# Moving the token scores and their softmax behind the output product, and transposing the memory 64 columns at a time, in a segmented memory-attention kernel

## The chip, the cores and the metric

The kernel runs on one core of one Trainium2 chip. The metric is the device time of one execution in microseconds (us): lower is better. The core's engines work at the same time, each through its own queue of instructions in order, and wait for one another by semaphores: TensorE (PE, with its weight loads shown apart as PEld), VectorE (DVE), ScalarE (ACT), GpSimd (POOL) and SyncE (SP), which issues most of the DMAs.

## The reference

Two blocks with a layernorm ahead of each and a residual around each: a memory-augmented attention that runs over segments in sequence, and a feed-forward block with a squared ReLU. Cut to what matters (S = 2048 tokens of width 640, 32 heads of 128, 8 memory rows, segments of 32 tokens, so 64 segments):

```python
for s in range(n_seg):
    h = concat([mem, x[s*32:(s+1)*32]])            # 8 memory rows and 32 tokens
    q, k, v = h @ Wq, h @ Wk, h @ Wv               # 32 heads
    scores = where(mask, q @ k.T * scale, -1e9)    # a memory row sees all 40, a token what is not behind it
    o = (softmax(scores) @ v) @ Wo
    mem = o[:8]                                    # feeds the next segment
    outs.append(o[8:])
h  = x + concat(outs)
h2 = h + relu(layernorm(h) @ w1 + b1)**2 @ w2 + b2
```

The eight memory rows of one segment's output are an input of the next segment, so the 64 segments form a chain.

## The kernel before, in words

All weights of the attention lie in SBUF. A block `b` is four segments; `step(b, sp)` does one segment `s = 4*b + sp`, 64 steps in all, and `for b ... for sp` at the end calls them. The order of the work on each engine is the order in which the code issues it (`tc.manual_schedule`): nothing is moved by a scheduler, so an instruction that waits holds up everything behind it on its engine.

A segment's rows are split. The memory rows and the first 24 tokens ("main", 32 rows) are projected in the step itself. The last 8 tokens of the four segments of a block ("tails") are projected ahead of time, as units of four matmuls kept in the list `fill`: ten units make one of q, k, v for a block, or (`wo_tail_units`) the output product of a block's tails. `run(fill, n)` issues the next n units; they also serve as work for TensorE while other engines finish something. `late`, `mid` and `win` are further lists: `late` holds work for the start of the next step (`flip`, the transpose of tail rows; `ln_stats`; the output of a tail product), `mid` layernorms, `win` 128-wide transposes on TensorE.

One step issues, in this order:

- up to three entries of `late`; on VectorE these stand ahead of the step's own transposes.
- `project`: q and k of head half 0, then of half 1 (20 matmuls each, L206), copied out by ScalarE (L222, L224, L403) and transposed into `qT` and `kT` by VectorE (`flip`, L227, and L406). `spread` copies the memory columns of `qT` into `qz` on GpSimd (L372, L374).
- `scores(0)` and `soft1(0)`: the memory rows' scores of half 0 (L414, L419) and the first part of their softmax. They read `qz` and `kT`.
- v of half 0 (`ps0`), with `token_scores(0)` (L487 the mask, L491) between its second and third chunk; then two chunks of v of half 1 (`ps1`), `scores(1)`, `token_scores(1)`, `soft1(1)`.
- `token_values` of the segment before (L353, L358), `values(0)` (L447, L452) and its copy by VectorE (L213), the remaining three chunks of `ps1`, `soft2(1)`, then on VectorE the token softmax's maximum `mxk` (L525) and difference `tk` (L527).
- the output product `pw` (`wo_rounds`, L238, 16 rounds of four matmuls): rounds 0 to 5, `values(1)` and its copy by ScalarE (L215), rounds 6 and 7, one unit of `fill`, rounds 8 to 15.
- the rest of the token softmax: `ek` (ScalarE, L540), `zk` and `rk` (VectorE, L542, L544), the products `pkt` and `pk` (GpSimd, L546, L549).
- `wo_out`: `otmp` (ScalarE, L245) and `o` (VectorE, L246); `token_out`: two copies by ScalarE (L363) and one by GpSimd (L365); `store_main`; an entry of `win`; four or six units of `fill`.
- `mem_to_hT`: the memory rows of `o` are transposed by 20 matmuls of 32 columns into `pm` (L316) and copied into the next step's `hT4` (VectorE, L318). The next step's projections wait for this.
- `tails_in`: GpSimd copies the next segment's tails into `qT` (L323) and `kT` (L325).
- two entries of `mid`, the rest of `fill`; then VectorE transposes `pkt` and `pk` (`pTt` L567, `pTk` L573) with two products on GpSimd between them (`pTx`, L570). The next step's `token_values` reads them.

The pools matter as follows. `mm` has three PSUM buffers, used in turn by every projection, by the token scores `sk` and by the units. `chn` has one, shared by `sm`, `pw` and `pm`. `rowtile` gives four row buffers in turn. The difference `tk` and `otmp` share one buffer (tag "tk").

After the steps comes the feed-forward part, in four blocks of 512 tokens (L813 to L857), which the change does not touch but for a buffer that it borrows earlier (`ht0[3]`).

Of the kernel before, what the change touches and what calls it, by code (L numbers as in the profile page):

```python
# [8 lines left out]
ACT = mybir.ActivationFunctionType  # L9
ALU = mybir.AluOpType  # L10
AX = mybir.AxisListType
F32 = mybir.dt.float32
BF16 = mybir.dt.bfloat16
# [3 lines left out]
def kernel(  # L17
# [16 lines left out]
    nc = tc.nc  # L34
    _, S, D = A_x.shape
    _, H, E = A_Wq.shape
    M = A_mem0.shape[1]
    SEG = 32
    G = 4
    HG = H // G  # L40
    HE = H * E
    EG = HE // G
    DC = D // 128
    DH = D // 2
    NB = S // 128
    NS = S // SEG
    HD = 24
    TL = SEG - HD
    NK = SEG + M
# [4 lines left out]
    scale = float(E) ** -0.5  # L54
# [13 lines left out]
    s1 = ctx.enter_context(tc.tile_pool(name="s1", bufs=1))  # L68
    s2 = ctx.enter_context(tc.tile_pool(name="s2", bufs=2))
# [5 lines left out]
    wv = wts.tile([128, DC * HE], BF16)  # L75
    wo = wts.tile([128, H, D], BF16)

    ident = const.tile([128, 128], BF16)
# [6 lines left out]
    mask = const.tile([128, HG, SEG], BF16)  # L85
# [15 lines left out]
    qT = const.tile([128, H, NK], BF16)  # L101
    kT = const.tile([128, H, 2 * SEG], BF16)
# [33 lines left out]
    for ch in range(2):  # L136
        nc.scalar.dma_start(out=o0[32 * ch:32 * ch + M, :].rearrange("m (c f) -> m c f", f=64),
                            in_=A_mem0[0].rearrange("m (c t f) -> t m c f", t=2, f=64)[ch])
# [22 lines left out]
    hT4s, hTts, tails = {}, {}, {}  # L161
# [34 lines left out]
    def proj(w, by, lhs, n, ps, c0, c1):  # L196

        if by == "columns":
            wr = w[:].rearrange("p (c g j n k e) -> p c n k g j e", c=DC, g=G, n=2, j=4, k=4)
        elif by == "half":  # L200
            wr = w[:].rearrange("p (c k j n e) -> p c n k j e", c=DC, k=G, n=2, j=4)
        else:
            wr = w[:].rearrange("p (c k n f) -> p c n k f", c=DC, k=G, n=2)
        for c in range(c0, c1):
            for k in range(4):
                nc.tensor.matmul(ps[32 * k:32 * k + 32, :], lhsT=lhs(c), rhs=wr[:, c, n, k], start=(c == 0), stop=(c == DC - 1))  # L206

    def mmtile():
        return mm.tile([128, 512], F32, tag="mm", name="ps")
# [31 lines left out]
    def wo_out(pw):  # L241
        o = o_ring[0]
        o_ring.append(o_ring.pop(0))
        tmp = s1.tile([128, DH], F32, tag="tk", name="otmp")
        nc.scalar.copy(out=tmp[0:64], in_=pw[64:128, 0:DH])  # L245
        nc.vector.tensor_tensor(out=o[0:64], in0=pw[0:64, 0:DH], in1=tmp[0:64], op=ALU.add)  # L246
        return o

    fill, late, mid, win = [], [], [], []

    def run(q, n):
        while n > 0 and q:
            q.pop(0)()
            n -= 1
# [57 lines left out]
    def mem_to_hT(o, hT4, sp):  # L312
        pm = chn.tile([128, 512], F32, tag="ch", name="pm")
        for c in range(DC):
            for q in range(4):
                nc.tensor.matmul(pm[32 * q:32 * q + 32, c * M:(c + 1) * M], lhsT=o[:, (2 * c + q % 2) * 32:(2 * c + q % 2 + 1) * 32],  # L316
                                 rhs=ident[:, q // 2 * 32:q // 2 * 32 + M], start=True, stop=True)
        nc.vector.tensor_copy(out=hT4[:, :, sp, 0:M], in_=pm[:, 0:DC * M].rearrange("p (c m) -> p c m", m=M))  # L318

    def tails_in(b, sp, which="qk", h0=0, h1=H):  # L320
        q, k = [tails[b][w][:].rearrange("p h (k s) -> p h s k", s=4)[:, h0:h1, sp, :] if w in which else None for w in "qk"]
        if "q" in which:
            nc.gpsimd.tensor_copy(out=qT[:, h0:h1, SEG:NK], in_=q)  # L323
        if "k" in which:
            nc.gpsimd.tensor_copy(out=kT[:, h0:h1, SEG:2 * SEG].rearrange("p h (j k) -> p h j k", k=TL),  # L325
                                  in_=k.unsqueeze(2).to_broadcast([128, h1 - h0, 4, TL]))
# [11 lines left out]
    def store_main(o, s):  # L338
        for ch in range(2):
            nc.sync.dma_start(out=o_all[s * SEG:s * SEG + HD, ch * DH:(ch + 1) * DH],  # L340
                              in_=o[32 * ch + M:32 * ch + 32, :])
# [19 lines left out]
    def token_out(s, po):  # L361
        for n in range(2):
            nc.scalar.copy(out=oTg[:, n, :, :, M:NK],  # L363
                           in_=po[:, :, n * 128:(n + 1) * 128].rearrange("p g (j q) -> p g j q", q=32))
        nc.gpsimd.tensor_copy(out=oTts[s // 4 % 2][:, :, s % 4 * TL:(s % 4 + 1) * TL], in_=oT[:, :, 32:NK])  # L365
# [12 lines left out]
    def step(b, sp, v=None):  # L378
        s = b * 4 + sp
        last = s == NS - 1  # L380
        hT4 = hT4s[b]
        lhs = lambda c: hT4[:, c, sp, :]
# [95 lines left out]
        if not ready:  # L478
            ps0 = mmtile()
            proj(wv, "half", lhs, 0, ps0, 0, 2)  # L480
        sk = mmtile()
        skv = sk[:, 0:HG * NK].rearrange("p (i k) -> p i k", k=NK)

        def token_scores(n):
            if n == 0:
                for g in range(G):
                    nc.tensor.matmul(skv[32 * g:32 * g + 32, :, M:NK], lhsT=ident[:, 0:32], rhs=mask[:],  # L487
                                     start=True, stop=False, skip_group_check=True)
            for j in range(4):
                for g in range(G):  # L490
                    nc.tensor.matmul(skv[32 * g:32 * g + 32, n * 4 + j, :], lhsT=qT[:, n * 16 + g * 4 + j, M:NK],  # L491
                                     rhs=kT[:, n * 16 + g * 4 + j, 0:NK], start=False, stop=(n == 1 and j == 3),
                                     skip_group_check=True)

        token_scores(0)
        if ready:
            run(fill, DC)
        if not ready:
# [3 lines left out]
            pT0 = soft2(0)  # L502
        if not ready:
            ps1 = mmtile()
            proj(wv, "half", lhs, 1, ps1, 0, 2)
        if not last:
            scores(1)
        token_scores(1)
        if not last:
            soft1(1)  # L510
        if ready:
            run(fill, DC)
        po = pop.tile([128, G, 512], F32, tag="po", name="po")
# [3 lines left out]
            values(0, pT0, po)  # L517
            values_out(0, po)
        if not ready:
            proj(wv, "half", lhs, 1, ps1, 2, DC)  # L520
            nc.scalar.copy(out=v[:, 512:1024], in_=ps1[:])  # L521
        if not last:
            pT1 = soft2(1)
        mxk = s1.tile([128, HG], F32, tag="mxk", name="mxk")
        nc.vector.tensor_reduce(out=mxk[:], in_=skv, op=ALU.max, axis=AX.X)  # L525
        tk = s1.tile([128, HG, NK], F32, tag="tk", name="tk")
        nc.vector.tensor_tensor(out=tk[:], in0=skv, in1=mxk[:].unsqueeze(2).to_broadcast([128, HG, NK]), op=ALU.subtract)  # L527

        pw = chn.tile([128, 512], F32, tag="ch", name="pw")
        main = lambda p: oT[:, p, 0:32]  # L530
        wo_rounds(main, pw, 0, 6)
        if not last:
            values(1, pT1, po)
            values_out(1, po)
        wo_rounds(main, pw, 6, 8)
        run(fill, 1)
        wo_rounds(main, pw, 8, 16)

        ek = s1.tile([128, HG, NK], BF16, tag="ek", name="ek")
        nc.scalar.activation(out=ek[:], in_=tk[:], func=ACT.Exp, scale=1.0)  # L540
        zk = s1.tile([128, HG], F32, tag="zk", name="zk")
        nc.vector.tensor_reduce(out=zk[:], in_=ek[:], op=ALU.add, axis=AX.X)  # L542
        rk = s1.tile([128, HG], F32, tag="rk", name="rk")
# [3 lines left out]
                                op=ALU.mult)  # L547
        pk = s1.tile([128, HG, 32], BF16, tag="pk", name="pk")
        nc.gpsimd.tensor_tensor(out=pk[:], in0=ek[:, :, 0:SEG], in1=rk[:].unsqueeze(2).to_broadcast([128, HG, SEG]),  # L549
                                op=ALU.mult)  # L550

        o = wo_out(pw)
        if s:
            token_out(s - 1, po)
        if s > 1:
            store_main(o, s - 2)
        outs = [win.pop(0)()] if win else []
        for f in outs:
            f()
        if not last:  # L560
            run(fill, 4 if outs else 6)
            mem_to_hT(o, hT4s[(s + 1) // 4], (s + 1) % 4)
            tails_in((s + 1) // 4, (s + 1) % 4)
        run(mid, 2)
        run(fill, 100)
        pTt = s1.tile([128, 2, 32], BF16, tag="pTt", name="pTt")
# [2 lines left out]
        for u in range(2):  # L569
            nc.gpsimd.tensor_tensor(out=pTx[:, u], in0=pTt[:, u, HD:32].unsqueeze(1).to_broadcast([128, 4, TL]),  # L570
                                    in1=same[:], op=ALU.mult)
# [39 lines left out]
    f1T = ck(FC * NT).rearrange("p (c t) -> p c t", c=FC)  # L611
    hnT0 = const.tile([128, DC, NT], BF16, name="hnT0")
    ht0 = [const.tile([128, D], BF16, name="ht0%d" % k) for k in range(NK4)]
    parked = [hnT0[:, c, :] for c in range(DC)] + [ht0[k][:, 0:512] for k in range(3)]
    hnTs = [hnT0[:], ck(DC * NT).rearrange("p (c t) -> p c t", c=DC)]
    ots = [ck(D) for _ in range(4)]
# [114 lines left out]
    for b in range(NB):  # L731
        for sp in range(4):
# [45 lines left out]
            if 2 <= e <= NK4 + 1:  # L778
                late.append(lambda e=e: prep_stats0(e - 2))
                mid.append(lambda e=e: prep_norm0(e - 2))  # L780
            step(b, sp, v0 if b + sp == 0 else None)

    def end_output(s):
# [10 lines left out]
    po = pop.tile([128, G, 512], F32, tag="po", name="po")  # L794
# [7 lines left out]
    for t in range(S // NT):  # L802
# [6 lines left out]
        for fc in range(FC):  # L809
            ps = mmtile()  # L810
            for c in range(DC):
                if fc < FFULL:
                    nc.tensor.matmul(ps[:], lhsT=w1[:, c, fc * 128:(fc + 1) * 128], rhs=hnT[:, c, :],  # L813
                                     start=(c == 0), stop=(c == DC - 1))
                    continue
                for hh in range(2):
                    nc.tensor.matmul(ps[FREM * hh:FREM * (hh + 1), 0:HT], lhsT=w1[:, c, fc * 128:F],
                                     rhs=hnT[:, c, HT * hh:HT * (hh + 1)], start=(c == 0), stop=(c == DC - 1))
# [4 lines left out]
            if more and fc >= 1 and (fc - 1) // 3 < NK4:  # L823
                k, stage = divmod(fc - 1, 3)
# [10 lines left out]
        for q in range(NK4):  # L835
# [6 lines left out]
            for hh in range(2):  # L842
                k = pr + 2 * hh
                for fc in range(FFULL):
                    nc.tensor.matmul(y[:, hh, 0:DH], lhsT=f1T[:, fc, k * 128:(k + 1) * 128], rhs=w2[:, fc, cs],  # L845
                                     start=(fc == 0), stop=False, skip_group_check=True)
                if more and q and (hh == 0 or q == 1):
                    k = q if hh == 0 and q > 1 else hh
                    prep_pe(t + 1, k, hn_[k])()
            for hh in range(2):  # L850
                r = slice(FREM * hh, FREM * (hh + 1))
                nc.tensor.matmul(y[:, hh, 0:DH], lhsT=f1T[r, FFULL, pr * 128:(pr + 1) * 128], rhs=w2[r, FFULL, cs],
                                 start=False, stop=True, skip_group_check=True)
# [40 lines left out]
```

## Time and profile before

| | |
|---|---|
| median of 3 runs | 1033.69 us (1029.55 to 1035.87) |
| the profiled execution's own time | 1031.81 us |
| its span, first to last instruction | 1029.7 us |
| granted TensorE clock, mean | 0.997 |
| PE busy | 970.4 us (94%) |
| DVE, ACT, POOL busy | 618.2 us, 533.9 us, 312.2 us |
| one step in the middle of the run | some 13 us |

How to read it: the profile is one execution on the chip. An instruction has a start and a duration; matmuls are pipelined, so a next one starts before the last has ended and the busy time counts both as one stretch. A group of instructions of one line, engine, operation and shape has a busy time, a mean duration in ns and the engine's idle time just before, with what ended it. In the timeline, "x20" are 20 instructions merged into one row, whose duration goes from the first's start to the last's end. A matmul's shape reads rows*columns of the stationary operand, then partitions x elements of the moving one: 128*32 128x512 takes 128 rows by 32 columns of weights. Line numbers are those of the listing above.

### The profile page before, as it was taken

The numbers are of one execution on the slowest core, as the hardware profiler recorded it, in microseconds if no ns is written. First come the engines' busy times: TensorE is split into PE (matmuls) and PEld (weight loads), VectorE is DVE, ScalarE is ACT, GpSimd is POOL, SyncE is SP. The second block draws the span as 40 slices with busy tenths as digits, with TensorE's granted clock in tenths as the row PEclk, the third lists the DMA queues.
The fourth block names the chain that finished last, engine by engine and source line by source line (L and its number), as shares of the span: only waits on it lengthen the run. The fifth ranks groups of instructions, "written<-read, shape, count | busy, mean of one in ns | idle before, by whom it ended". The sixth has DMA issues, their size and how long they took to land.

```text
span 1029.7 us, 58960 instructions
## 1 busy us (share of the span) xinstructions
PE 970.4 (94%) x26951; PEld 573.9 (56%) x26960; DVE 618.2 (60%) x1740; ACT 533.9 (52%) x1229; POOL 312.2 (30%) x807
## 2 busy tenths in 40 slices
PE   5779899999999999999999999999999999999998
PEld 2345455655655555565655665555566565555555
DVE  2156666766666766666666666666666676466432
ACT  3336555555555655555655555555555555533431
POOL 1123333333333333333333232323332333433210
PEclk9999999999999999999999999999999999999999
DMA  9960101000101010000000000000000110612200
GB/s 356 385 193 26 23 7 31 7 25 6 35 7 29 7 36 12 22 15 26 16 22 14 19 23 14 22 14 26 15 21 8 47 34 7 208 50 65 77 26 26
DMA packets 39144, 51.58 MB, mean 50 GB/s; under 512 B 6192, under 2 KB 34992, under 8 KB 36976
## 3 DMA queue, kind: packets, MB, share of 16 engines
q1 hardware_dynamic: 37936, 47.29, 13.9%
q8 instruction: 210, 3.44, 1.4%
q0 software_dynamic: 320, 0.26, 0.1%
q14 instruction: 38, 0.31, 0.1%
q10 hardware_dynamic: 640, 0.27, 0.1%
HBM read 38.37 MB, written 9.44 MB: 46 GB/s over the span
## 4 chain that ended last, share of the span: by engine, by line
PE 86%; DMA 6%; issue 2%; DVE 2%; SPq 2%; ACT 1%; ACTq 0%; DVEq 0%; POOL 0%; POOLq 0%
PE ps L206 47%; PE pw L238 15%; PE y L845 5%; PE ps L813 4%; PE ps L238 3%; PE po L447 2%; PE po L353 2%; PE sm L419 2%; DMA wq<-in_B_w_dram 1%; DMA vt_d<-row 1%; SPq L146 1%; DMA wv<-in_A_Wv_dram 1%; PE ps L491 1%; DMA wo<-in_A_Wo_dram 1%; PE pm L316 1%
## 5 line engine op out<-in xcount | busy, mean ns | idle before, releaser
L206 PEld LDWEIGHTS <-hT 128*32 128x32 bf16 x7680 | 193.2, 96 | 183.6 <-issue 19.6
L238 PE MATMUL pw<-wo,oT 128*32 128x320 bf16 x4224 | 185.2, 300 | 8.0 <-issue 3.6
L206 PE MATMUL ps<-wv,hT 128*32 128x512 bf16 x2520 | 171.3, 379 | 3.1 <-issue 2.5
L206 PE MATMUL ps<-wq,hT 128*32 128x512 bf16 x2520 | 159.2, 381 | 4.9 <-DVE hT L318 4.9
L206 PE MATMUL ps<-wk,hT 128*32 128x512 bf16 x2520 | 158.6, 380 | 0.1
L238 PEld LDWEIGHTS <-oT 128*32 128x32 bf16 x4224 | 106.7, 96 | 59.2 <-issue 12.1
L222 ACT ACTIVATE row<-ps 128x512 bf16<-128x512 f32 x156 | 93.3, 599 | 75.0 <-PE ps L206 74.5
L227 DVE STREAM_TRANSPOSE qT<-row 128x512 bf16<-128x512 bf16 x128 | 90.3, 705 | 65.8 <-ACT row L222 65.7
L546 POOL TENSOR_TENSOR pkt<-ek,rk 128x64 bf16<-128x64 bf16 x64 | 19.0, 296 | 360.6 <-DVE rk L544 360.6
L224 ACT CAST row<-ps 128x512 bf16<-128x512 f32 x115 | 68.0, 591 | 31.5 <-PE ps L206 31.3
L372 POOL COPY qz<-qT 128x96 bf16<-128x96 bf16 x126 | 33.7, 267 | 138.2 <-DVE qT L227 136.3
L325 POOL COPY kT<-kTt 128x1024 bf16<-128x1024 bf16 (+1 forms) x65 | 71.9, 1106 | 10.6 <-DVE kTt L227 10.6
L206 PEld LDWEIGHTS <-hTt 128*32 128x32 bf16 x1920 | 54.0, 97 | 32.1 <-issue 2.6
L245 ACT COPY otmp<-pw 64x320 f32<-64x320 f32 x66 | 27.9, 423 | 82.4 <-PE pw L238 82.4
L363 ACT CAST oT<-po 128x512 bf16<-128x512 f32 x128 | 68.7, 589 | 1.6
L246 DVE TENSOR_TENSOR o<-pw,otmp 64x320 bf16<-64x320 f32 x66 | 31.8, 482 | 62.5 <-ACT otmp L245 62.5
L521 ACT CAST v<-ps 128x512 bf16<-128x512 f32 x63 | 36.9, 586 | 60.7 <-PE ps L206 60.7
L227 DVE STREAM_TRANSPOSE kT<-row 128x512 bf16<-128x512 bf16 x65 | 46.1, 709 | 32.1 <-ACT row L224 32.1
L542 DVE TENSOR_REDUCE zk<-ek 128x8 f32<-128x320 bf16 x64 | 31.1, 486 | 50.9 <-ACT ek L540 50.9
L845 PE MATMUL y<-wq,wk 128*128 128x320 bf16 x416 | 61.2, 299 | 0.2
L403 ACT CAST row<-ps 128x256 bf16<-128x256 f32 x126 | 40.7, 375 | 30.0 <-PE ps L206 30.0
L500 ACT CAST v<-ps 128x512 bf16<-128x512 f32 x63 | 36.9, 586 | 30.3 <-PE ps L206 30.3
(114 smaller groups left out, 1630.2 us busy)
## 6 DMA issues: line engine op xcount, KB each, us to landing
wv<-in_A_Wv_dram SPq DMA_DIRECT2D x5, 1024.0 KB
wq<-in_A_Wq_dram SPq DMA_DIRECT2D x5, 1024.0 KB
wk<-in_A_Wk_dram SPq DMA_DIRECT2D x5, 1024.0 KB
vt<-vt_d SPq DMA_DIRECT2D x60, 64.0 KB
xt<-in_A_x_dram SPq DMA_DIRECT2D x20, 160.0 KB
vt_d<-row SPq DMA_DIRECT2D x22, 128.0 KB
wo<-in_A_Wo_dram SPq DMA_DIRECT2D x2, 1280.0 KB
wo<-in_A_Wo_dram SPq DMA_DIRECT2D x4, 640.0 KB
```

Source lines behind the costliest of these rows:

```text
L206: nc.tensor.matmul(ps[32 * k:32 * k + 32, :], lhsT=lhs(c), rhs=wr[:, c, n, k], start=(c == 0), stop=(c == DC - 1))
L222: nc.scalar.mul(out=row, in_=ps, mul=scale)
L224: nc.scalar.copy(out=row, in_=ps)
L227: nc.vector.transpose(out=dst[:, n * 16:(n + 1) * 16, 0:32], in_=row.rearrange("p (h e) -> p h e", e=32))
L238: nc.tensor.matmul(pw[32 * j:32 * j + 32, 0:DH], lhsT=lhs(p), rhs=wov2[:, head(p), ch], start=(h == 0), stop=(h == 15))
L325: nc.gpsimd.tensor_copy(out=kT[:, h0:h1, SEG:2 * SEG].rearrange("p h (j k) -> p h j k", k=TL), in_=k.unsqueeze(2).to_broadcast([128, h1 - ...
L363: nc.scalar.copy(out=oTg[:, n, :, :, M:NK], in_=po[:, :, n * 128:(n + 1) * 128].rearrange("p g (j q) -> p g j q", q=32))
L403: nc.scalar.copy(out=row[:, u * 256:(u + 1) * 256], in_=ps[:, u * 256:(u + 1) * 256])
L500: nc.scalar.copy(out=v[:, 0:512], in_=ps0[:])
L521: nc.scalar.copy(out=v[:, 512:1024], in_=ps1[:])
L813: nc.tensor.matmul(ps[:], lhsT=w1[:, c, fc * 128:(fc + 1) * 128], rhs=hnT[:, c, :], start=(c == 0), stop=(c == DC - 1))
L845: nc.tensor.matmul(y[:, hh, 0:DH], lhsT=f1T[:, fc, k * 128:(k + 1) * 128], rhs=w2[:, fc, cs], start=(fc == 0), stop=False, skip_group_chec ...
```

## The change

- `mem_to_hT`: ten matmuls with 64 columns of weights each, in place of 20 with 32.
- The token scores of both halves are issued together, behind `values(1)` and rounds 6 and 7 of the output product, where one unit of `fill` stood; that unit is now issued behind the output product with the others. `ps1` issues three chunks ahead of `scores(1)` and two behind `values(0)` (before: two and three).
- `mxk` and `tk` follow the token scores. `tk` has a buffer of its own, borrowed from `ht0[3]` and later from the pool of tail columns.
- `ek` stands behind `otmp` and ahead of `token_out` on ScalarE. `tails_in` stands ahead of the units and `mem_to_hT`. `zk`, `rk`, `pkt` and `pk` stand behind `mem_to_hT`, so on GpSimd behind `token_out`'s copy and `tails_in`, and on VectorE behind the copy of `pm`.

```diff
     def mem_to_hT(o, hT4, sp):
         pm = chn.tile([128, 512], F32, tag="ch", name="pm")
         for c in range(DC):
-            for q in range(4):
-                nc.tensor.matmul(pm[32 * q:32 * q + 32, c * M:(c + 1) * M], lhsT=o[:, (2 * c + q % 2) * 32:(2 * c + q % 2 + 1) * 32],
-                                 rhs=ident[:, q // 2 * 32:q // 2 * 32 + M], start=True, stop=True)
+            for ch in range(2):
+                nc.tensor.matmul(pm[64 * ch:64 * ch + 64, c * M:(c + 1) * M], lhsT=o[:, c * 64:(c + 1) * 64],
+                                 rhs=ident[:, 32 * ch:32 * ch + M], start=True, stop=True)
...
-        sk = mmtile()
-        skv = sk[:, 0:HG * NK].rearrange("p (i k) -> p i k", k=NK)
-
-        def token_scores(n):
...
+        def token_scores(skv):
...
-        token_scores(0)
...
-            proj(wv, "half", lhs, 1, ps1, 0, 2)
+            proj(wv, "half", lhs, 1, ps1, 0, 3)
         if not last:
             scores(1)
-        token_scores(1)
-        if not last:
             soft1(1)
...
-            proj(wv, "half", lhs, 1, ps1, 2, DC)
+            proj(wv, "half", lhs, 1, ps1, 3, DC)
             nc.scalar.copy(out=v[:, 512:1024], in_=ps1[:])
         if not last:
             pT1 = soft2(1)
-        mxk = s1.tile([128, HG], F32, tag="mxk", name="mxk")
-        nc.vector.tensor_reduce(out=mxk[:], in_=skv, op=ALU.max, axis=AX.X)
-        tk = s1.tile([128, HG, NK], F32, tag="tk", name="tk")
-        nc.vector.tensor_tensor(out=tk[:], in0=skv, in1=mxk[:].unsqueeze(2).to_broadcast([128, HG, NK]), op=ALU.subtract)
...
         wo_rounds(main, pw, 6, 8)
-        run(fill, 1)
+        sk = mmtile()
+        skv = sk[:, 0:HG * NK].rearrange("p (i k) -> p i k", k=NK)
+        token_scores(skv)
+        mxk = s1.tile([128, HG], F32, tag="mxk", name="mxk")
+        nc.vector.tensor_reduce(out=mxk[:], in_=skv, op=ALU.max, axis=AX.X)
+        if s == NS - 7:
+            tks.append(s2.tile([128, 2 * HG * NK], BF16, tag="hTt", name="tk")[:])
+        tk = tks[-1].bitcast(F32).rearrange("p (i k) -> p i k", k=NK)
+        nc.vector.tensor_tensor(out=tk, in0=skv, in1=mxk[:].unsqueeze(2).to_broadcast([128, HG, NK]), op=ALU.subtract)
         wo_rounds(main, pw, 8, 16)
-
+        o = wo_out(pw)
         ek = s1.tile([128, HG, NK], BF16, tag="ek", name="ek")
-        nc.scalar.activation(out=ek[:], in_=tk[:], func=ACT.Exp, scale=1.0)
+        nc.scalar.activation(out=ek[:], in_=tk, func=ACT.Exp, scale=1.0)
+        if s:
+            token_out(s - 1, po)
+        if s > 1:
+            store_main(o, s - 2)
+        if not last:
+            tails_in((s + 1) // 4, (s + 1) % 4)
+        outs = [win.pop(0)()] if win else []
+        for f in outs:
+            f()
+        if not last:
+            run(fill, 4 if outs else 6)
+            mem_to_hT(o, hT4s[(s + 1) // 4], (s + 1) % 4)
         zk = s1.tile([128, HG], F32, tag="zk", name="zk")
...
-        o = wo_out(pw)
-        if s:
-            token_out(s - 1, po)
-        if s > 1:
-            store_main(o, s - 2)
-        outs = [win.pop(0)()] if win else []
-        for f in outs:
-            f()
-        if not last:
-            run(fill, 4 if outs else 6)
-            mem_to_hT(o, hT4s[(s + 1) // 4], (s + 1) % 4)
-            tails_in((s + 1) // 4, (s + 1) % 4)
         run(mid, 2)
         run(fill, 100)
...
+    tks = [ht0[3][:]]
```

More of the change, by code (lines that the diff above doesn't have):

```diff
@@ L480, in step @@
             proj(wv, "half", lhs, 0, ps0, 0, 2)
-        sk = mmtile()
-        skv = sk[:, 0:HG * NK].rearrange("p (i k) -> p i k", k=NK)
-        def token_scores(n):
-            if n == 0:
-                for g in range(G):
[L487 to L492, printed above, removed]
+        def token_scores(skv):
+            for g in range(G):
+                nc.tensor.matmul(skv[32 * g:32 * g + 32, :, M:NK], lhsT=ident[:, 0:32], rhs=mask[:],
+                                 start=True, stop=False, skip_group_check=True)
+            for i in range(HG):
+                n, j = i // 4, i % 4
+                for g in range(G):
+                    nc.tensor.matmul(skv[32 * g:32 * g + 32, i, :], lhsT=qT[:, n * 16 + g * 4 + j, M:NK],
+                                     rhs=kT[:, n * 16 + g * 4 + j, 0:NK], start=False, stop=(i == HG - 1),
                                      skip_group_check=True)
-        token_scores(0)
         if ready:
```

## The prediction

> **What bounds the kernel now.** I read the page first: busy times, then the chain that ended last.
>
> ```profile
> PE 970.4 (94%) x26951; PEld 573.9 (56%) x26960; DVE 618.2 (60%) x1740; ACT 533.9 (52%) x1229; POOL 312.2 (30%) x807
> ...
> PE 86%; DMA 6%; issue 2%; DVE 2%; SPq 2%; ACT 1%; ACTq 0%; DVEq 0%; POOL 0%; POOLq 0%
> ```
>
> TensorE sets the time: 94% busy, 86% of the chain. The other engines have slack on average, but every step has places where TensorE needs what they have just made. So I took one step out of the timeline, engine by engine, and measured from W, the start of the last matmul of the output product. TensorE first (508.13 + 0.84 less the 0.299 of one matmul gives W = 508.67):
>
> ```profile
> 508.13 0.84 PE L238 MATMUL pw<-wo,oT 128*32 128x320 bf16 x17
> 508.73 1.53 PE L206 MATMUL ps<-wk,hTt 128*32 128x512 bf16 x24
> 510.06 0.29 PE L316 MATMUL pm<-ident,o 128*32 128x8 bf16 x19
> ...
> 515.18 0.19 PE L419 MATMUL sm<-kT,qz 128*32 128x64 bf16 x2
> ```
>
> `scores(0)` (L419) start at W+6.51 (6.54 in most steps of this kind). They need the first q and k flips of VectorE:
>
> ```profile
> 510.47 0.20 DVE L318 CAST hT<-pm 128x40 bf16<-128x40 f32 x1 [0.47 <-PE pm L316]
> 510.59 0.23 DVE L567 STREAM_TRANSPOSE pTt<-pkt 128x64 bf16<-128x64 bf16 x1
> 510.74 0.40 DVE L573 STREAM_TRANSPOSE pTk<-pk 128x256 bf16<-128x256 bf16 x1
> 511.11 1.30 DVE L227 STREAM_TRANSPOSE kTt<-row 128x512 bf16<-128x512 bf16 x2
> 512.78 0.71 DVE L227 STREAM_TRANSPOSE qT<-row 128x512 bf16<-128x512 bf16 x1 [0.37 <-ACT row L222]
> 513.85 0.71 DVE L227 STREAM_TRANSPOSE kT<-row 128x512 bf16<-128x512 bf16 x1 [0.35 <-ACT row L224]
> ```
>
> The k flip ends at 514.56, 0.6 us before its use. That slack is the number to keep. `pTt` and `pTk` stand ahead of all flips and wait for nobody, since GpSimd has made `pkt` and `pk` long before:
>
> ```profile
> 508.83 0.30 POOL L546 TENSOR_TENSOR pkt<-ek,rk 128x64 bf16<-128x64 bf16 x1 [5.23 <-DVE rk L544]
> 509.09 0.62 POOL L549 TENSOR_TENSOR pk<-ek,rk 128x256 bf16<-128x256 bf16 x1
> 510.64 0.40 POOL L365 COPY oTt<-oT 128x256 bf16<-128x256 bf16 x1 [0.94 <-ACT oT L363]
> 510.98 0.42 POOL L323 COPY qT<-qTt 128x256 bf16<-128x256 bf16 x1
> 511.35 1.12 POOL L325 COPY kT<-kTt 128x1024 bf16<-128x1024 bf16 x1
> ```
>
> **The change part by part.** *Token softmax behind the tails.* In the changed order GpSimd does L365, L323, L325 and only then `pkt` and `pk`; VectorE does the copy of `pm`, `zk`, `rk`, then `pTt` (waits for `pkt`), `pTk` (waits for `pk`), then the flips. ScalarE does `otmp`, `ek`, then `token_out`:
>
> ```profile
> 509.06 0.42 ACT L245 COPY otmp<-pw 64x320 f32<-64x320 f32 x1 [1.13 <-PE pw L238]
> 509.51 1.07 ACT L363 CAST oT<-po 128x512 bf16<-128x512 f32 x2
> ```
>
> `token_out` ends at W+1.91 now. `ek` (0.473 by its group's mean) goes ahead of it: W+2.38, or W+2.28 if its start overlaps by 0.10 as successive ScalarE instructions do at L363 (two of 0.589 in 1.07). L365 starts 0.06 later; from its start to the end of L325 it is 1.83 (510.64 to 512.47); then `pkt` 0.26 to the start of `pk`, and 0.62; then 0.03 for the semaphore and 0.40 for `pTk`. VectorE is free at W+5.43 to W+5.57; I take 5.5 against 2.48 now. `zk` and `rk` (0.49 + 0.20 after the copy of `pm`, some W+2.7) and the layernorms of `mid` (0.6) lie beside this and cost nothing; without that cover they would cost their 0.7 us.
>
> Behind `pTk` on VectorE stand the entries of `late`, the q flip and the k flip. Back to back the latter two take 1.25 (0.64 to the next start, 0.71 less an overlap), and 0.04 passes to TensorE. TensorE for its part arrives at 6.54 + 0.22 (the unit of `fill` now behind the product, one round of four matmuls: the six rounds at 508.73 start some 0.22 apart) + 0.18 (shapes, below) = W+6.9. By the kind of step that follows:
>
> - two tail flips in `late` (1.27): 5.5 + 1.27 + 1.25 + 0.04 = W+8.06, so `scores(0)` come 1.52 later than now.
> - `ln_stats` in `late` (0.93 from the end of `pTk` to the next flip, in a step at 863 us): W+7.72, against 6.54 where ten units fill the end and 6.38 where five do: 1.18 and 1.34 later.
> - a tail product's `o` (0.45): W+7.2, before TensorE arrives: no wait.
>
> *The rest of the step, `scores(0)` to W.* The token scores are the same 36 matmuls: 0.21 + 0.11 now, 0.32 together. The unit that leaves the product takes 0.22 out. One chunk of v (0.22) and `token_scores(1)` (0.11) no longer stand between `scores(1)` and the product's start. `values(0)` begin 0.11 earlier, and from their last matmul's start (505.24) to the end of the VectorE copy L213 (505.82) and its semaphore it takes 0.64; two chunks (0.43) and a shape change (0.11 from start to start) cover 0.55. A new wait of 0.09. Sum: -0.22 + 0.09 = -0.13 a step. `values(1)` keep some 0.2 of slack; the copy L215 is covered by the token scores, 0.31 where the unit gave 0.22. `mxk` and `tk` (0.94) end 0.15 before `otmp`. SP's queue holds only `store_main` here, in unchanged order.
>
> *Memory transposes.* 20 matmuls take 0.13 us (510.06 to 510.19): either 6.5 ns each, and ten take 0.065, or 26 ns a round on each column strip, and the five rounds remain. The saving is 0 to 0.065; I take 0. (The Trainium skill, TensorEngine Tiling (Array Packing), section Instruction Overhead, says each matmul has about 60 cycles of overhead, so that one column costs what 60 do; by that five rounds remain and nothing is saved.) Against it stands the new shape, 128*64 among 128*32. The feed-forward part shows a change of width and back:
>
> ```profile
> 913.69 1.03 PE L813 MATMUL ps<-hnT,wq 128*128 128x512 bf16 x4
> 914.64 0.74 PE L817 MATMUL ps<-hnT,wq 128*64 128x256 bf16 x10
> 915.31 0.58 PE L845 MATMUL y<-wq,wk 128*128 128x320 bf16 x3
> ```
>
> L813's last start is 914.34, and L817 comes 0.30 later where 0.216 is the spacing; back, 0.21 where 0.107 is. So 0.09 a change, two a step: 0.18, from 0 (a narrower change may cost nothing) to 0.20. (The same page, section Key Properties, says that changing the tiling mode drains the engine; by that the 0.18 is paid, and the trace agrees with 0.09 each.) Where TensorE waits at `scores(0)` anyway, this is inside the wait.
>
> **Sum.** 28 steps behind tail flips: 1.52 - 0.13 = 1.4 each, 39.2. Three of them have `ln_stats` too, 2.7 more. Nine times 1.21 and five times 1.05 for `ln_stats` alone: 16.1. Thirteen steps without a wait: 0.18 + 0.09 = 0.27 each, 3.5. The seven at the ends, likewise: some 4.5. Together +66 us. On the profiled execution's own 1031.8 (span 1029.7 and 2.1 around it) this is 1098; the median of the runs is 1.9 higher.
>
> **The rivals.** *(1) The late flips find cover, and only small costs remain* (chance 0.13): if GpSimd's spans, rough in any profile, are shorter than shown, VectorE must be free by W+6.9-0.04-1.25-1.27 = 4.3 for no wait. Then each of 63 steps pays 0.27: 1049. Against it: L365 to L325 takes 1.8 to 1.95 in every steady step. *(2) Not slower* (0.07): the chain ends by 4.3 and the narrower shape change is free as well. Then half the transposes save 0.065 x 64 = 4, and ten steps with five units, where TensorE waits for `o`, gain their unit's 0.22: some 1026. It needs 1.2 us off a chain whose instructions are all in the trace. *(3) A second wait at `scores(1)`* (0.12): behind a late k flip come the q flip (0.64), `mx`, and two k flips, ending 1.6 after it; `scores(1)` come 1.88 after it. Above 0.25 more, say GpSimd's `qz` late behind `pTx`, and 40 steps pay 0.5 each: 1118. *The transposes as such doing nothing* is already in my sum.
>
> **How the numbers follow.** The forecast (0.68) is 1098, its own range 1079 to 1110: 0.07 either way on 49 steps, and below by up to 15, as the 15.5 us that TensorE idles by "issue" may go into the new waits. The range reaches towards (1) and over (3): 1062 to 1118. The runs before spread by 6 us, so about 1% (10 us) can be told from no change. Faster by more than that 0.03, within it 0.06 (the rest of (2) and a little of (1)), slower 0.91.
>
> **What would show it.** In the changed profile: `pkt` waiting not for `rk` but starting as L325 ends; `pTt` idle behind `pkt`; no gap between `pTk` and the flips; TensorE idle some 1.2 us at L419 in steps behind tail flips and about none at a block's first step; L213 ahead of L238 with 0.1; L316 preceded and followed by 0.09. I am wrong if VectorE's flips start where they do now, or if L419 shows no idle time.

## The result, and the profile after

The changed kernel takes 1098.73 us (median of 4 runs, 1095.19 to 1099.2) against 1032.01 before; the ratio is 1.0636, with a 95% interval of 1.0614 to 1.0658. The median before moved between 1027 and 1035 us from one batch of runs to another, so below every kernel is given with its ratio to the kernel before in the same batch.

The page of the changed kernel, busy times and the chain that ended last:

```profile
span 1097.1 us, 57756 instructions
...
PE 996.7 (91%) x26320; PEld 584.2 (53%) x26320; DVE 606.2 (55%) x1740; ACT 538.4 (49%) x1229; POOL 309.4 (28%) x807
...
PE 30%; issue 30%; POOL 17%; DVE 13%; DMA 4%; ACT 4%; SPq 2%; POOLq 0%; ACTq 0%; DVEq 0%
```

GpSimd and VectorE, almost absent from the chain before, now hold 30% of it, although neither is busier: what was beside TensorE's work is now ahead of it. The other 30%, "issue", is not TensorE's: in the step below it is a stretch of 7.6 us ahead of L365, for which the walk back along the chain finds no releaser, while the timeline puts it down to ScalarE. TensorE's own pauses by "issue" are 15.6 us over the run in both kernels. The same place as in the prediction, one step, W = 544.46 (543.90 + 0.86 less 0.30). GpSimd, in the timeline (start, us, engine, line):

```profile
546.76 0.40 POOL L365 COPY oTt<-oT 128x256 bf16<-128x256 bf16 x1 [7.63 <-ACT oT L363]
...
547.47 1.12 POOL L325 COPY kT<-kTt 128x1024 bf16<-128x1024 bf16 x1
548.53 0.31 POOL L557 TENSOR_TENSOR pkt<-ek,rk 128x64 bf16<-128x64 bf16 x1
548.78 0.63 POOL L560 TENSOR_TENSOR pk<-ek,rk 128x256 bf16<-128x256 bf16 x1
```

`pkt` starts as the copy of `kT` ends, not when `rk` is there (547.18). VectorE:

```profile
546.98 0.20 DVE L555 RECIPROCAL rk<-zk 128x8 f32<-128x8 f32 x1
548.87 0.25 DVE L565 STREAM_TRANSPOSE pTt<-pkt 128x64 bf16<-128x64 bf16 x1 [1.69 <-POOL pkt L557]
549.45 0.45 DVE L571 STREAM_TRANSPOSE pTk<-pk 128x256 bf16<-128x256 bf16 x1 [0.33 <-POOL pk L560]
549.82 1.26 DVE L227 STREAM_TRANSPOSE kTt<-row 128x512 bf16<-128x512 bf16 x2
551.00 0.67 DVE L227 STREAM_TRANSPOSE qT<-row 128x512 bf16<-128x512 bf16 x1
551.59 0.67 DVE L227 STREAM_TRANSPOSE kT<-row 128x512 bf16<-128x512 bf16 x1
```

VectorE stands 1.69 + 0.33 us at `pTt` and `pTk`, and the four flips follow with no gap. The k flip ends at 552.26, W+7.80. TensorE:

```profile
543.90 0.86 PE L238 MATMUL pw<-wo,oT 128*32 128x320 bf16 x19
...
545.99 0.32 PE L316 MATMUL pm<-ident,o 128*64 128x8 bf16 x10
...
551.43 0.19 PE L414 MATMUL sm<-bmask,ident 128*32 128x32 bf16 x4
552.32 0.30 PE L419 MATMUL sm<-kT,qz 128*32 128x64 bf16 x16 [0.69 <-DVE kT L227]
```

`scores(0)` issue the mask at 551.43 and then wait for that flip until 552.32. Over the run, the longest waits of TensorE (us in total, times, longest):

```profile
PE sm L419 <- POOL qz L372: 23.1, 21, 2.0
PE sm L419 <- DVE kT L227: 17.5, 25, 1.0
PE ps L489 <- issue: 12.6, 20, 0.9
...
PE ps L206 <- DVE o L246: 5.8, 14, 1.2
```

Of the 21 waits put down to `qz`, 19 are in steps behind `ln_stats`: there GpSimd's layernorm products stand ahead of `qz`, and they wait for `ln_stats`, which stands behind `pTk` on VectorE. In these steps `qz` and the k flip end within 0.02 us of each other, so both are late from one cause. From the start of the mask to the first of L419, summed over `scores(0)` of all segments but the first and the last, TensorE spends 49.9 us, where before it was 2.3.

### The profile page after: what moved, and what is told of

It is laid out like the page before. It is cut to its first block, busy times and chain, and to the rows that moved or that the text cites. A ratio compares the mean times of both kernels' runs of the same rounds, so it can differ in the third digit from the quotient of the medians.

```text
span 1097.1 us, 57756 instructions
## 1 busy us (share of the span) xinstructions
PE 996.7 (91%) x26320; PEld 584.2 (53%) x26320; DVE 606.2 (55%) x1740; ACT 538.4 (49%) x1229; POOL 309.4 (28%) x807
## 4 chain that ended last, share of the span: by engine, by line
PE 30%; issue 30%; POOL 17%; DVE 13%; DMA 4%; ACT 4%; SPq 2%; POOLq 0%; ACTq 0%; DVEq 0%
PE ps L206 9%; PE pw L238 6%; POOL kT L325 6%; PE y L844 5%; PE ps L812 5%; DVE qT L227 4%; POOL pk L560 3%; POOL oTt L365 2%; DVE pTk L571 2%; ACT oT L363 2%; DVE lnst L153 2%; DVE kTt L227 2%; DVE qTt L227 2%; DVE kT L227 1%; POOL pkt L557 1%
## 5 line engine op out<-in xcount | busy, mean ns | idle before, releaser
L206 PEld LDWEIGHTS <-hT 128*32 128x32 bf16 x7680 | 199.4, 97 | 198.9 <-issue 24.9
L238 PE MATMUL pw<-wo,oT 128*32 128x320 bf16 x4224 | 183.5, 301 | 7.6 <-DMA wo<-in_A_Wo_dram 2.9
L206 PE MATMUL ps<-wq,hT 128*32 128x512 bf16 x2520 | 159.0, 381 | 8.7 <-DVE o L246 5.4
L365 POOL COPY oTt<-oT 128x256 bf16<-128x256 bf16 x64 | 25.8, 402 | 479.6 <-ACT oT L363 479.6
L206 PE MATMUL ps<-wk,hT 128*32 128x512 bf16 x2520 | 158.6, 380 | 0.8 <-DVE o L246 0.4
L206 PE MATMUL ps<-wv,hT 128*32 128x512 bf16 x2520 | 159.0, 380 | 0.0
L238 PEld LDWEIGHTS <-oT 128*32 128x32 bf16 x4224 | 102.3, 96 | 52.8 <-DVE oT L213 25.0
L227 DVE STREAM_TRANSPOSE qT<-row 128x512 bf16<-128x512 bf16 x128 | 86.3, 675 | 23.3 <-ACT row L222 23.3
L531 DVE TENSOR_REDUCE mxk<-ps 128x8 f32<-128x320 f32 x64 | 31.5, 492 | 111.8 <-PE ps L489 111.8
L419 PE MATMUL sm<-kT,qz 128*32 128x64 bf16 x2016 | 38.9, 193 | 40.7 <-POOL qz L372 23.1
L428 ACT ACTIVATE em<-sm,mx 128x64 bf16<-128x64 f32 x126 | 39.9, 316 | 72.4 <-DVE mx L425 72.4
L206 PEld LDWEIGHTS <-hTt 128*32 128x32 bf16 x1920 | 53.8, 98 | 35.4 <-issue 3.1
L565 DVE STREAM_TRANSPOSE pTt<-pkt 128x64 bf16<-128x64 bf16 x64 | 15.7, 246 | 97.7 <-POOL pkt L557 97.7
L419 PEld LDWEIGHTS <-qz 128*32 128x32 bf16 x2016 | 28.1, 95 | 60.1 <-POOL qz L372 49.4
```

Source lines behind the costliest of these rows:

```text
L227: nc.vector.transpose(out=dst[:, n * 16:(n + 1) * 16, 0:32], in_=row.rearrange("p (h e) -> p h e", e=32))
L238: nc.tensor.matmul(pw[32 * j:32 * j + 32, 0:DH], lhsT=lhs(p), rhs=wov2[:, head(p), ch], start=(h == 0), stop=(h == 15))
L419: nc.tensor.matmul(sm[32 * g:32 * g + 32, 0:2 * SEG], lhsT=qz[:, p, :], rhs=kT[:, p, :], start=False, stop=(j == 3), skip_group_check=True)
L428: nc.scalar.activation(out=em[:], in_=sms[n][:, 0:2 * SEG], func=ACT.Exp, bias=mx[:, 0:1], scale=1.0, accum_out=zm[:])
```

## The experiments

Theory G is the prediction's: GpSimd makes `pkt` and `pk` only behind the tails' copies, VectorE waits for them at the head of its queue, and the flips behind are late for `scores(0)`. Rival S says that the shape of the 64-column transposes is the cost, rival P that the token scores inside the output product are.

**The tails' copies behind `pk` again** (on the changed kernel).

```diff
         if s > 1:
             store_main(o, s - 2)
-        if not last:
-            tails_in((s + 1) // 4, (s + 1) % 4)
...
         nc.gpsimd.tensor_tensor(out=pk[:], ...
+        if not last:
+            tails_in((s + 1) // 4, (s + 1) % 4)
```

> The changed kernel with one step moved back: the tails' copies into qT and kT stand behind pkt and pk on GpSimd. Theory G (GpSimd makes pkt and pk only after 1.8 us of copies, VectorE stands at pTt and pTk, and the flips behind them are late): pTk ends at W+4.1 instead of W+5.4, scores(0) wait in hardly any step, and the 46 us at L419 and the 8 us at q of half 1 go: 1045, range 1038 to 1052. Rival S (the 64-column transposes, which drain TensorE twice a step, are the cost) and rival P (the token scores inside the output product are): the time stays above 1080.

1042.11 us, ratio 1.0115 (1.0098 to 1.0131). `pTk` ends at W+4.2, and TensorE spends 7.7 us between mask and L419 in place of 49.9. What is left in its waits there:

```profile
PE sm L419 <- POOL qz L372: 4.0, 6, 1.9
```

The wait for `o` fell from 5.8 us to 0.2 as well. One moved step takes the loss from 6.4% to 1.2%, so S and P cannot be the main cost.

**`pTt`, `pTx` and `pTk` in the next step** (on the changed kernel). This leaves GpSimd late and takes the wait out of VectorE's way.

```diff
         project("q", wq, qT, 0)
         if not last and not ready:
             spread(0)
         if not last:
             project("k", wk, kT, 0)
+        if s:
+            token_transposes()      # pTt, pTx, pTk of the step before
...
-        pTt = s1.tile(...)          # to back.append((pTk, pTx)), at the end of the step
```

> The changed kernel with pTt, pTx and pTk issued in the next step, behind the first k flip; GpSimd still does the tails ahead of pkt and pk. Theory G says that it is VectorE's order that turns late products into late flips, so the wait at L419 goes although pkt and pk stay late: 1045, range 1038 to 1052. If GpSimd itself were the bound (its copies of qT into qz late behind pkt and pk), the time would stay near 1098. Rivals S and P: near 1098.

1037.63 us, ratio 1.0068 (1.0053 to 1.0083), just under the range given. One step of it, W = 565.80, GpSimd and then VectorE:

```profile
568.80 1.11 POOL L325 COPY kT<-kTt 128x1024 bf16<-128x1024 bf16 x1
569.87 0.29 POOL L572 TENSOR_TENSOR pkt<-ek,rk 128x64 bf16<-128x64 bf16 x1
570.12 0.61 POOL L575 TENSOR_TENSOR pk<-ek,rk 128x256 bf16<-128x256 bf16 x1
```

```profile
568.55 1.51 DVE L227 STREAM_TRANSPOSE kTt<-row 128x512 bf16<-128x512 bf16 x2
570.52 0.71 DVE L227 STREAM_TRANSPOSE qT<-row 128x512 bf16<-128x512 bf16 x1 [0.46 <-ACT row L222]
571.51 0.71 DVE L227 STREAM_TRANSPOSE kT<-row 128x512 bf16<-128x512 bf16 x1 [0.28 <-ACT row L224]
572.14 0.20 DVE L463 STREAM_TRANSPOSE pTt<-pkt 128x64 bf16<-128x64 bf16 x1
```

`pk` ends at W+4.93, as late as in the changed kernel (W+4.95), but the k flip now ends at W+6.42 and nobody waits for it. So it is not GpSimd's lateness that costs: it is that VectorE waits for it ahead of the flips.

**The softmax behind the tails alone** (on the kernel before: `zk` to `pk` moved behind `tails_in`, all else as before).

```diff
-        zk = s1.tile(...)           # to pk, ahead of o = wo_out(pw)
...
             mem_to_hT(o, hT4s[(s + 1) // 4], (s + 1) % 4)
             tails_in((s + 1) // 4, (s + 1) % 4)
+        zk = s1.tile(...)           # to pk
```

> The kernel before with one part of the change alone: zk, rk, pkt and pk behind mem_to_hT and the tails' copies; token scores, ek, transposes as before. Theory G: pTk at W+5.1 (ek does not delay token_out here), scores(0) 1.2 us late behind tail flips, 0.8 to 1.0 behind ln_stats, 0.65 at a block's first step: 1082, range 1070 to 1090. Rivals S and P, of which nothing is in this kernel: 1027 to 1037.

1094.27 us, ratio 1.0613 (1.0595 to 1.0631). With neither the 64-column transposes nor the moved token scores in it, this part alone loses nearly what the whole change does. In a step with W = 540.7 the queue of VectorE looks as in the changed kernel:

```profile
544.79 0.25 DVE L566 STREAM_TRANSPOSE pTt<-pkt 128x64 bf16<-128x64 bf16 x1 [1.46 <-POOL pkt L558]
545.36 0.45 DVE L572 STREAM_TRANSPOSE pTk<-pk 128x256 bf16<-128x256 bf16 x1 [0.33 <-POOL pk L561]
545.73 1.26 DVE L227 STREAM_TRANSPOSE kTt<-row 128x512 bf16<-128x512 bf16 x2
```

The delays that I listed came: `scores(0)` start at W+7.53 to 7.68 in most steps behind tail flips (7.71 expected), 7.35 behind `ln_stats`, 7.69 in a block's first step. Their sum over the run is 58.7 us by the profile. My total of 1082 was 12 us too low and the time lies above the range: the delays as listed come to some 57, and I had written a smaller sum. The loss by the medians is 63.7 us; the 5 us that are not in these delays were not followed.

**The 32-column transposes again** (on the changed kernel: the first hunk of the diff undone).

> The changed kernel with the 20 transposes of 32 columns again. Theory G: the two shape changes a step lie inside waits for VectorE in nearly every step, so it saves 0 to 3 us: 1096 to 1099. Rival S: 63 steps times 0.2 us or more: 1086 or less.

1094.81 us, ratio 1.0623 (1.0606 to 1.0639), which isn't told apart from the changed kernel's 1.0636. The us lie just under the range, but the kernel before was 1.4 us faster in this batch too; by the ratios the saving is some 1.3 us. TensorE's waits in it:

```profile
PE sm L419 <- POOL qz L372: 24.3, 21, 2.0
PE sm L419 <- DVE kT L227: 23.5, 25, 1.1
```

Together 47.8 us where the changed kernel has 40.6, and the wait for `o` at L206 is 9.8 where it has 5.8: what the transposes save is waited away at these two places. The price of the shape is hidden here, not absent, as the next run shows.

**The 64-column transposes alone** (on the kernel before: the first hunk of the diff alone).

> The kernel before with the ten 64-column transposes alone. In the changed kernel's trace the step into the transposes takes 0.104 more and the transposes with the step out 0.125 more than before (0.254 against 0.129). Theory G with this price: some 47 of the 63 steps have TensorE busy on both sides and pay 0.23, so +11 on some 1031: 1042, range 1038 to 1045. If the shapes cost nothing and half the instructions save time: 1026 to 1030.

1040.48 us, ratio 1.0127 (1.0111 to 1.0142): 13 us slower. The weight loads of L316 are, in the changed kernel's trace and then in that of the kernel before (duration in ns, least, median, most):

```profile
L316 PEld LDWEIGHTS <-o x640: 106/113/158, 8.2 to 945.0; 128*64 128x64 bf16 x160
L316 PEld LDWEIGHTS <-o x1280: 92/93/113, 8.7 to 879.0; 128*32 128x32 bf16 x183
```

A weight load takes 113 ns for 64 columns against 93 for 32, and from the first start to the last ten of these matmuls take 0.151 us where twenty of the old took 0.114. Whether the longer load is why was not tried. The step into them takes 0.104 longer, they and the step out 0.125 longer. Half the instructions, and 0.23 us more a step.

**The tail product's buffer** (on the changed kernel). The wait for `o` at L206 was not in my prediction. A block's first step in the changed kernel, TensorE and then VectorE:

```profile
563.08 1.25 PE L206 MATMUL ps<-wk,hT 128*32 128x512 bf16 x20
564.67 1.26 PE L206 MATMUL ps<-wq,hT 128*32 128x512 bf16 x20 [0.34 <-DVE o L246]
```

```profile
563.81 0.45 DVE L571 STREAM_TRANSPOSE pTk<-pk 128x256 bf16<-128x256 bf16 x1 [0.33 <-POOL pk L560]
564.18 0.44 DVE L246 TENSOR_TENSOR o<-ps,otmp 64x320 bf16<-64x320 f32 x1
```

q of half 1 starts 1.59 after k of half 0, where 1.08 is the spacing, and it starts when `o` has read the tail product from the `mm` buffer. That is at W+5.79 (W = 558.83). Before the change `o` waited only for ScalarE and ended at W+3.95 (W = 522.03):

```profile
525.50 0.48 DVE L246 TENSOR_TENSOR o<-ps,otmp 64x320 bf16<-64x320 f32 x1 [0.82 <-ACT otmp L245]
```

The experiment frees that buffer by ScalarE alone:

```diff
-        nc.vector.tensor_tensor(out=o[0:64], in0=pw[0:64, 0:DH], in1=tmp[0:64], op=ALU.add)
+        low = pw[0:64, 0:DH]
+        if both:                    # of a tail product
+            tm2 = tks[-1].bitcast(F32)
+            nc.scalar.copy(out=tm2[0:64], in_=low)
+            low = tm2[0:64]
+        nc.vector.tensor_tensor(out=o[0:64], in0=low, in1=tmp[0:64], op=ALU.add)
```

> The changed kernel, with the tail product's PSUM buffer freed by ScalarE alone: it copies both halves to SBUF and VectorE adds from there. If the 0.54 us that TensorE loses at q of half 1 in each block's first step is that buffer, held by VectorE's o behind pTk, the 8 us at that place go and nothing else moves: 1091, range 1088 to 1094. If it is something else (a row buffer, ScalarE): no change, 1098.

1084.65 us, ratio 1.0547 (1.0528 to 1.0566): 0.9% under the changed kernel, some 9 us where 8 were expected. The us lie under the range, since the kernel before was 5 us faster in this batch. The wait for `o` at L206 is gone from the trace, and these steps now come to `scores(0)` 0.38 later than before the change in place of 0.9. From one W to the next the thirteen of them take 0.8 us more than before the change, where in the changed kernel it is 9.5.

**What is left of the change without these costs.** First the late `pTt` and `pTk` with the 32-column transposes, then in addition two chunks of v of half 1 ahead of `scores(1)` as before the change.

> pTt, pTx and pTk behind the first k flip, and the 20 transposes of 32 columns: what is left of the change are the token scores inside the output product and the order on GpSimd. With 0.23 a step for the shapes: 11 below the 1037.6 of the kernel with 64 columns: 1027, range 1023 to 1031, so the moved token scores themselves cost nothing. Rival P (moving the token scores costs as such): 1033 or more.

> As the kernel before this one, with two chunks of v of half 1 ahead of scores(1) and three behind values(0), as the kernel before the change had it. The wait of TensorE for L213 ahead of the output product (0.067 a step) goes, and scores(1) come 0.22 earlier after scores(0), for which the k flips leave some 0.4: 4 us less than that kernel, 1023, range 1019 to 1027. If the k flips are then late, it is no faster than that kernel.

The first takes 1021.66 us, ratio 0.9947 (0.9932 to 0.9962), the second 1019.15, ratio 0.9914 (0.99 to 0.9929): 0.5% and 0.9% under the kernel before, and clearly faster than the changed one. The first lies just under its range, but the kernel before was 3 us faster in this batch than in that of the second experiment; the chunk gave 0.3%, some 3 us, where 4 were expected. So P falls too. The 64-column shape is worth 12 us between the second experiment and the first of these. The chunk is worth 0.067 us a step at the start of the output product: from the last v matmul to L238 it is 0.273 in the first (as in the changed kernel) and 0.206 in the second (as before).

**Whether the late transposes are the gain** (on the kernel before: only `pTt`, `pTx`, `pTk` behind the first k flip).

> The kernel before with pTt, pTx and pTk behind the first k flip and nothing else. There they wait for nobody, and the flips ahead of which they stood have 0.6 us to spare: 0, within 0.4% of before. If the 8 us that the kernel with the moved token scores, 32-column transposes and two chunks is ahead of before come from this move alone, it is 0.9% faster.

1035.63 us, ratio 0.9991 (0.9979 to 1.0004): nothing, as they waited for nobody there.

**The three edits without moving `pTt` and `pTk`**: the tails' copies behind `pk`, 32-column transposes, two chunks.

> The changed kernel with the tails' copies behind pkt and pk, the 20 transposes of 32 columns and two chunks of v ahead of scores(1); pTt and pTk where the change has them. Against the kernel with pTt and pTk moved instead (0.991 of before) it pays the few waits that are left behind tail flips and ln_stats together and in single steps, some 4 us: 0.991 to 0.997 of before. So the whole loss of the change would be undone by these three edits, with the token scores where the change put them.

1032.95 us, ratio 0.9974 (0.996 to 0.9988), just outside the range. The loss is undone, but it is 0.6% behind the version with the late transposes, more than the 4 us that I gave it. Its `pTk` ends at W+4.1 to 4.2 in most steps and thirteen steps still wait: between mask and L419 TensorE spends 7.1 us, against 3.3 in the version with the late transposes. That is the 4 us; the remaining 2 are about as wide as the intervals, and what they are stays open.

Where the best version gains its 0.9%, some 9 us, on the kernel before is not shown. The wait for `o` at L316 is 5.3 us (6 times) in its trace and 6.6 (11 times) before, as one may expect from the unit that now stands behind the product. The pauses of TensorE that the profile calls "issue" are 8.2 us in its trace and 15.6 before, but these two traces come from different batches. The kernel with the 64-column transposes alone, of the same batch as the best version, has only 9.9 with the token scores where they were, so their shrinking can't be put down to the moved token scores.

## Why the prediction was right

1098 was forecast and 1098.73 measured. The mechanism held at each link. The first four rows are of the step shown, the others are medians over the steps:

| | forecast | measured |
|---|---|---|
| `token_out` ends, us after W | 2.28 to 2.38 | 2.23 |
| `pTk` ends | 5.43 to 5.57 | 5.44 |
| TensorE arrives at `scores(0)` (the mask) | 6.9 | 6.97 |
| `scores(0)` behind tail flips | 8.06 | 7.86 |
| `scores(0)` behind `ln_stats` | 7.72 | 7.71 |
| L213 ahead of L238, new wait a step | 0.09 | 0.067 |
| step into the transposes | 0.09 more | 0.104 more |

(The terms listed for `pTk` add up to 5.48 to 5.58, not 5.43 to 5.57; nothing hangs on it.) The signs that it named came, one of them smaller: behind tail flips TensorE stands 0.9 us between mask and L419 in the step shown, not 1.2.

The total is nearer than its terms by luck, because two errors cancel. By kind of step, from one W to the next, in us over the profiled run:

| steps behind | forecast | measured |
|---|---|---|
| tail flips, 25 | 35 | 28.1 |
| tail flips and `ln_stats`, 3 | 6.9 | 7.9 |
| `ln_stats`, five units, 9 | 10.9 | 12.4 |
| `ln_stats`, ten units, 5 | 5.3 | 3.8 |
| a tail product's `o`, 13 | 3.5 | 9.5 |
| the seven at the ends | 4.5 | 4.5 |

*Too high: the tail flips.* `scores(0)` come 1.37 later than before and not 1.52, since four flips in a row start 0.59 apart and not 0.64. The rest of these steps is 0.25 shorter and not 0.13; the pauses by "issue" sit in other places (at the token scores, 12.6 us, where before they were at `values` and the product), but their sum is the same, so I leave that open.

*Too low: "a tail product's `o`: no wait".* I followed VectorE only to `scores(0)`. Its `o` also frees one of three `mm` buffers, which q of half 1 needs. It stood behind `pTk` too, and TensorE lost some 0.5 us in each of these steps. The experiment on the buffer showed it.

*The transposes.* I took no saving and 0.18 for the shape; measured are 0.23, of which 0.104 is the step in, 0.088 the step out and 0.04 the matmuls themselves. (The Trainium skill's page TensorEngine Tiling (Array Packing), section Key Properties, says that a change of tiling mode drains the engine: 0.104 into the transposes agrees with it.) As foreseen, the price lies inside the wait wherever TensorE waits at L419, so it shows only once that wait is gone.

Of the rivals, (1) would have needed shorter GpSimd spans; they were as shown. (2) falls with the 64-column run, 13 us slower. (3), a second wait at `scores(1)`, did not come: from `scores(0)` to `scores(1)` steps behind tail flips take 0.01 longer than before, and those behind `ln_stats` 0.09.

## What to carry to other kernels

Where an engine's queue is in order, a wait costs what stands behind it, not what it waits for: before a producer is moved later, list what the waiting instruction blocks, and either move the wait behind those or keep the producer early. Follow each late instruction to all that it frees, buffers as well as data. Half as many, wider matmuls need not save time: here they took longer than the narrow ones, and each change of the array's shape cost 0.1 us besides.

## What the runs showed of the hardware that I had not expected

Ten tiny matmuls with 64 columns of weights took longer (0.151 us from first to last start) than twenty with 32 (0.114), besides 0.1 at each change of shape. VectorE's 128x512 flips take 0.71 alone but start 0.59 apart when they follow one another.
